# Attention and LayerNorm MLP on one Trainium2 core: the first pair's keys moved to SyncE's queue, the weights g spread in three pieces, and the first attention's list sorted anew

## The chip, the core and the metric

The kernel runs on one core of a Trainium2 chip. A core has five engines, each with its own list of instructions that it works through in order: TensorE (PE in the profile, with its weight loads apart as PEld), VectorE (DVE), ScalarE (ACT), GpSimd (POOL) and SyncE (SP). Engines wait for each other through semaphores. DMA transfers are issued by an engine (SyncE, ScalarE or GpSimd; the profile writes SPq, ACTq, POOLq) into that engine's queue. Operands lie in SBUF, results of matmuls in PSUM.

The metric is the device time of one execution in microseconds (us), as the median over runs of the same kernel.

## The reference

```python
B, H, S, D = 8, 12, 448, 64          # q, k, v: (8, 12, 448, 64) float32; x: (8, 448, 768)
def rmsnorm(x, g):
    return x / sqrt(mean(x * x, -1) + 1e-06) * g
q_n, k_n = rmsnorm(q, g_q), rmsnorm(k, g_k)
attn = softmax(q_n @ k_n.T / sqrt(64))            # per head
x = (attn @ v), heads side by side                # (8, 448, 768)
xn = (x - mean(x)) / sqrt(var(x) + 1e-06) * g_ln
out = x + relu(xn @ w_ch1) @ w_ch2                # w_ch1 768 x 3072, w_ch2 3072 x 768
```

## The kernel before

Heads are worked on in pairs, six pairs to a batch, pairs 0 to 47 in all. Pairs are prepared in units: units 0 to 3 hold pairs 0, 1, 2-3 and 4-5 (batch 0), unit 4 pairs 6-7, and so on; unit 8 holds pairs 14-15. A head's 448 rows are three times 128 "main" rows and 64 "left" rows; the left rows of a pair's two heads share one tile.

**Preparing a pair.** For queries and keys: squares (ScalarE, `square`, L113 and L551), their sums (VectorE, L504), the root (ScalarE, L494/L495), the scaling (VectorE, L515 for keys, L562 for queries). g_q and g_k are only ever used as the product g_q*g_k, `gprod`, which is multiplied onto one side (L555 for the queries of batch 0, the qG steps, and L263 for later keys). Keys are split into a high fp16 half and a low one (steps j and k; L105/L107 and L522), queries are doubled (step m or qm, a copy qn, L568), so that a score is a product of high and low parts at once. Keys and queries are then turned: by TensorE into the PSUM tile `tr` (K steps, L331/L334; Q steps, L348/L351; batch 0's queries into `psQ`, L581), from which a copy brings them to SBUF (C and D steps, QC steps), or by a DMA transpose (steps x and y, L287/L290 for keys and L297/L300 for queries). `tr` exists once: the next K or Q step needs the copy of the one before to be over. Values are cast to fp16 on GpSimd (steps z; L605/L610, later L311/L317).

**Scores, exponentials, values.** S steps are score matmuls, E steps the exponentials on ScalarE (L404, in batch 0 L647), V steps exponentials times values (L441/L443, in batch 0 L668). In batch 0 these go over blocks of query columns, phases 0, 1 and 2 (`S1.3.0` is phase 1, pair 3, half 0; `Q_PARTS` lists which pairs' queries are prepared together); for later pairs `S8.4` is pair 8, seventh part 4. O and T steps scale by the sums and collect the LayerNorm's statistics.

**The MLP.** A and N steps normalise 128 rows, X steps transpose them into `xnT`, U steps are up-projection matmuls of batch 0 (L692, `psU`) and R steps their relu (L700/L702); H steps are the down-projection (L1026, `psC`), J adds x, P stores. For later batches the up-projection is at L992 (`psH`) with its relu at L994. The weights w_ch1 come in three thirds (W0, W1, W2; L899) and w_ch2 in two halves (W3, W4; L904), each issued by GpSimd behind a tiny copy (`poke`, L778) that waits for a load of the inputs. The steps named Y belong to the LayerNorm of batch 1 (Y.X: its DMA transposes, L974).

**What sets the order.** For batch 0's attention and MLP and for batch 1's attention (pairs 6 to 11), with the preparation that lies among them, the order on every engine is the hand-written list `ORDER`: `first_attention` walks it and issues each step to its engine. The table `ENGINE` says which engine does a step that several could do (A ScalarE, V VectorE, P GpSimd; anything not named has a default: VectorE for copies out of PSUM by `moved`, GpSimd for the products qG). `F22` is 22 filler matmuls (L818, `psW`), which multiply the identity with itself and whose result nobody reads. From there on `run_rest` interleaves the MLP of batch b with the attention of batch b + 1 by a planner.

**The loads at the start** are issued ahead of the list, in `load_first`. `key(eng, p)` issues pair p's main key rows on engine `eng`'s queue, `load_left` the left rows (two DMAs, one for each head), `main` queries or values on SyncE's. Before, ScalarE issues pair 0's main keys, pair 0's left rows and pair 1's main keys; SyncE pair 0-1's queries, g_q and g_k (into `gg`), and then the rest; GpSimd the left rows of pairs 1 to 5, after it has built the identity matrix (`make_identity`) for the transposes. `spread_g` multiplies g_q and g_k in one partition (L737), spreads the product over 128 partitions by a matmul with ones (L739, `psG`) and copies it back (L740); it is the first step of `ORDER`.

Of the kernel before, what the change touches and what calls it, by code (L numbers as in the profile page):

```python
# [21 lines left out]
NPAIR = H // 2  # L22
# [5 lines left out]
ENGINE = dict(x.split(":") for x in """ j1:P C1:A QC0.0:A qG0.2:V QC0.2:A QC1.3:A qG2.0:V  # L28
qG2.4:V qm2.4:P QC2.4:A R0.3:V R0.4:V R0.5:V R1.4:V R1.5:V XC2:A R2.0:V R2.2:V R2.4:V c4:P j4:P
m4:P i5:V m5:P j6:P a7:P i7:V j7:P m7:P c8:V j8:P m8:P""".split())  # L30
# [3 lines left out]
spread a0 d0 qa0.0 h0 qt0.0 a1 qG0.0 n0 j0 qg0.0 d1 k0 ql0.0 G L4k qm0.0 h1 F22 K0 n1 a2 C0  # L34
Q0.0 j1 qa1.0 k1 d2 qa0.2 QC0.0 qt0.2 F12 K1 L4q F12 S0.0.0 h2 qt1.0 n2 E0.0.0 a3 C1 L4v qg0.2
j2 S0.0.1 qG0.2 d3 ql0.2 E0.0.1 F30 S0.1.0 h3 qg1.0 qG1.0 qm0.2 F20 Q0.2 E0.1.0 k2 n3 F6 K2
QC0.2 S0.1.1 C2 E0.1.1 ql1.0 j3 F13 S0.2.0 qm1.0 K3 k3 E0.2.0 C3 qa2.0 qt2.0 F7 Q1.3 S0.2.1
Q1.0 E0.2.1 F8 K4 S0.3.0 z0 S0.3.1 W0 V0.0 qa2.4 QC1.3 C4 E0.3.1 F4 K5 qt2.4 qg2.0 QC1.0 E0.3.0
S0.4.0 C5 qG2.0 V0.1 z3 E0.4.0 S0.4.1 qg2.4 E0.4.1 z2 ql2.0 qm2.0 F4 S0.5.0 L5k V0.2 E0.5.0 L5q
F5 S0.5.1 qG2.4 E0.5.1 ql2.4 V0.3 S1.0.0 V0.4 S1.0.1 E1.0.0 V0.5 S1.1.0 Q2.2 E1.0.1 E1.1.0  # L40
S1.1.1 O0.0 T0.0 L6k S1.2.0 W1 O0.1 Q2.0 E1.1.1 E1.2.0 S1.2.1 S1.3.0 V1.0 E1.2.1 S1.3.1 E1.3.0
E1.3.1 V1.1 S1.4.0 S1.4.1 V1.2 E1.4.0 E1.4.1 QC2.0 S1.5.0 V1.3 E1.5.0 T0.1 G2 S1.5.1 V1.4 A0
S2.0.0 E1.5.1 E2.0.0 N0 X0 QC2.2 L5v b4 a4 XC0 S2.0.1 L6v V1.5 qm2.4 O1.0 S2.0.2 O1.1 c4 T1.0
E2.0.2 U0.0 S2.1.0 d4 e4 E2.0.1 V2.0 Q2.4 R0.0 E2.1.0 S2.1.1 S2.1.2 T1.1 QC2.4 E2.1.2 E2.1.1
U0.1 S2.2.0 S2.2.1 g4 A1 V2.1 E2.2.0 S2.2.2 E2.2.1 N1 X1 E2.2.2 l4 S2.3.0 E2.3.0 V2.2 XC1 i4
# [21 lines left out]
BEHIND = {0: (4, 1), 2: (5, 2), 3: (6, 2), 4: (7, 2)}  # L67
PE_SET = (DMA_UNIT + 1) % 2
EARLY = {9: (89, 97)}
PIECES = {x + str(u) for x in "bacdegijklmzxy" for u in range(4, 9)}  # L70
LN_EXP_SET = 6
TWO_LEFT = 5
REC_LO, REC_HI = 1.0 / 3.0e7, 0.5
# [1231 lines left out]
```

## Time and profile before

| | |
|---|---|
| time, median of 3 runs | 598.51 us (597.85 to 599.85) |
| the profiled execution | 599.46 us, of it 597.9 us from the first to the last instruction (span) |
| TensorE busy | 582.4 us, 97% |
| VectorE, ScalarE, GpSimd busy | 296.7, 351.1, 186.2 us |
| granted TensorE clock, mean | 0.999 |

A profile row of the timeline reads: start in us, length in us, engine, line of the kernel, operation, output<-input by the program's names, shapes and types, how many instructions are put together (x3), and in brackets how long the engine had idled before it and whose work ended that. A group's row reads: busy us and mean ns of one, then the idle time before. A matmul's own length includes its way through the array, so that a row's length is more than its distance to the next. Line numbers of the kernel after the change lie a few lines further down (L171 becomes L172, L728 becomes L731).

### The profile page before, as it was taken

To read this page: it belongs to the slowest core of one execution; us is meant where nothing else is said; L and a number is where in the kernel's file an instruction comes from. 1 tells how busy PE (TensorE), PEld (TensorE's weight loads), DVE (VectorE), ACT (ScalarE), POOL (GpSimd) and SP (SyncE) were. 2 spreads that over 40 slices of the span, in tenths; PEclk is the share of its full clock that TensorE was granted. 3 is DMA by queue.
4 is the path that set the end of the run, shared out by engine and by line. 5 is a ranking of instruction groups with operands and counts; after the bars stand their busy time and mean duration, and the time that the engine had idled before them with its cause. 6 is when DMAs were issued, how large, how long until landed. Compare 5 with 4: busy or idle time off the path is not lost.

```text
span 597.9 us, 12462 instructions
## 1 busy us (share of the span) xinstructions
PE 582.4 (97%) x4999; PEld 362.9 (61%) x4999; DVE 296.7 (50%) x645; ACT 351.1 (59%) x668; POOL 186.2 (31%) x250
## 2 busy tenths in 40 slices
PE   5899999999999999999999999999999999999997
PEld 4789886545565666654566656654566666654565
DVE  6999997344455355724256255733356322450011
ACT  5899772188852797358843598538765387114300
POOL 3737251025650555232642345414412000000000
PEclk9999999999999999999999999999999999999999
DMA  8999999727996666946956496749623320040011
GB/s 268 220 243 206 221 230 175 197 51 132 123 178 142 135 96 153 173 128 82 152 130 134 85 125 144 189 105 142 120 63 90 93 63 1 27 107 0 1 53 56
DMA packets 130225, 75.25 MB, mean 126 GB/s; under 512 B 96468, under 2 KB 120356, under 8 KB 130164
## 3 DMA queue, kind: packets, MB, share of 16 engines
q1 hardware_dynamic: 113092, 44.53, 37.5%
q0 software_dynamic: 16128, 29.27, 23.6%
q8 instruction: 40, 0.66, 0.5%
q10 hardware_dynamic: 944, 0.62, 0.4%
q14 instruction: 21, 0.17, 0.1%
HBM read 52.30 MB, written 11.01 MB: 106 GB/s over the span
## 4 chain that ended last, share of the span: by engine, by line
PE 89%; DVE 4%; SPq 2%; ACT 2%; DMA 2%; issue 1%; POOL 0%; POOLq 0%; DVEq 0%
PE psC L1026 36%; PE psH L992 30%; PE psS L383 8%; PE oA L441 5%; PE psU L692 3%; PE oB L443 2%; PE psS L389 1%; SPq L297 1%; PE psS L636 1%; DMA qU<-qn 1%; DMA w<-in_g_k_dram 1%; PE oA L668 1%; PE tr L334 1%; DVE khl L522 0%; ACT E L404 0%
## 5 line engine op out<-in xcount | busy, mean ns | idle before, releaser
L1026 PE MATMUL psC<-w,hT 128*128 128x384 f16 (+1 forms) x1368 | 234.9, 323 | 0.0
L992 PE MATMUL psH<-xnT,w 128*128 128x512 f16 (+1 forms) x1008 | 218.1, 356 | 0.0
L404 ACT ACTIVATE E<-psS,rr_all 128x448 f16<-128x448 f32 x273 | 170.9, 637 | 51.9 <-PE psS L383 50.1
L1026 PEld LDWEIGHTS <-hT 128*128 128x128 f16 x1368 | 127.2, 98 | 78.9 <-issue 4.3
L994 ACT ACTIVATE hT<-psH 128x512 f16<-128x512 f32 (+1 forms) x168 | 93.8, 559 | 129.5 <-PE psH L992 127.8
L992 PEld LDWEIGHTS <-w 128*128 128x128 f16 x1008 | 91.1, 98 | 76.9 <-issue 2.3
L383 PE MATMUL psS<-qU,kU 128*128 128x448 f16 x252 | 86.5, 352 | 1.1 <-DMA qU<-qn 0.5
L441 PEld LDWEIGHTS <-E 128*128 128x128 f16 x819 | 56.3, 98 | 36.1 <-issue 1.6
L1033 DVE SCALAR_TENSOR_TENSOR x<-psC,rs_all,x 128x384 f32<-128x384 f32 x48 | 29.2, 615 | 76.4 <-PE psC L1026 75.9
L263 POOL TENSOR_TENSOR qkv<-qkv,gprod 128x896 f32<-128x896 f32 x18 | 37.7, 2095 | 85.4 <-ACT khl L113 70.0
L441 PE MATMUL oA<-v,E 128*128 128x65 f16 x756 | 58.1, 193 | 0.1
L454 DVE RECIPROCAL rec_all<-oA 128x6 f32<-128x6 f32 x42 | 8.2, 195 | 86.0 <-PE oA L441 85.5
L163 POOL DMA_DIRECT2D qkv<-in_k_dram x14 | 11.2, 797 | 123.6 <-ACT E L404 73.4
L443 PE MATMUL oB<-v,E 128*128 128x65 f16 x252 | 45.3, 193 | 0.1
L255 DVE TENSOR_REDUCE ssq<-khl 128x14 f32<-128x896 f32 x21 | 22.7, 1082 | 44.4 <-ACT khl L113 44.4
L383 PEld LDWEIGHTS <-kU 128*128 128x128 f16 x252 | 24.3, 98 | 17.5 <-issue 1.2
L88 DVE SCALAR_TENSOR_TENSOR qn<-qkv,rr_all 128x256 f16<-128x256 f32 (+2 forms) x71 | 25.2, 415 | 16.9 <-ACT rr_all L259 16.9
L255 DVE TENSOR_REDUCE ssq<-qn 128x14 f32<-128x896 f32 x21 | 22.8, 1084 | 21.3 <-ACT qn L113 21.3
L692 PE MATMUL psU<-xnT,w 128*128 128x128 f16 x432 | 27.1, 219 | 0.0
L443 PEld LDWEIGHTS <-E 128*128 128x128 f16 x273 | 26.3, 96 | 0.4 <-DVE xl L461 0.4
L692 PEld LDWEIGHTS <-w 128*128 128x128 f16 x432 | 25.3, 98 | 1.4 <-issue 0.2
L456 DVE TENSOR_TENSOR x<-oA,rec_all 128x384 f32<-128x384 f32 x42 | 23.4, 558 | 1.3
(160 smaller groups left out, 604.8 us busy)
## 6 DMA issues: line engine op xcount, KB each, us to landing
out_dram<-x SPq DMA_DIRECT2D x20, 384.0 KB, 2.5
qkv<-in_v_dram POOLq DMA_DIRECT2D x15, 384.0 KB, 7.5
qkv<-in_k_dram POOLq DMA_DIRECT2D x14, 384.0 KB, 3.8
qkv<-in_q_dram POOLq DMA_DIRECT2D x14, 384.0 KB, 5.6
w<-in_moe_w_ch_dram POOLq DMA_DIRECT2D x3, 1536.0 KB, 12.5
w<-in_moe_w_ch_dram POOLq DMA_DIRECT2D x2, 2304.0 KB, 25.3
qkv<-in_q_dram SPq DMA_DIRECT2D x7, 384.0 KB, 11.3
qkv<-in_v_dram SPq DMA_DIRECT2D x6, 384.0 KB, 5.8
```

The source lines that it names most:

```text
L88: nc.vector.scalar_tensor_tensor(out=out, in0=x, scalar=8.0, in1=r.unsqueeze(2).broadcast_to([x.shape[0], g, D]), op0=ALU.mult, op1=ALU.mult)
L255: nc.vector.tensor_reduce(out=c["ssq"][:, n], in_=c["sq", n], axis=AX.X, op=ALU.add)
L263: _on(nc, f"i{u}", "P").tensor_tensor(out=self.loads[u][1], in0=self.loads[u][1], in1=sh.gprod.unsqueeze(1).broadcast_to([128, g, D]), op= ...
L383: nc.tensor.matmul(ps[0][:, 0:S], c["main"][:, ts(i, 128)], c["q"][:, ts(h, S)], start=True, stop=True)
L404: self.nc.scalar.activation(out=o, in_=c.pop(("ps", i))[:, 0:S], func=AFT.Exp, scale=self.units[u][3][:, g:g + 1], bias=EXP_BIAS)
L441: nc.tensor.matmul(oA[:, t, cs], E[:, ts(t, 128)], rhs, start=(i == 0 and t == 0), stop=(i == 6 and t == 2))
L443: nc.tensor.matmul(oB[:, cs], E[:, 320:448], rhs, start=(i == 0), stop=(i == 6))
L692: nc.tensor.matmul(ps[:, ts(f, 128)], sh.w1[:, dc, ts(4 * k + f, 128)], self.xnT[:, dc, ts(t, 128)], start=(f == 0 and dc == 0), stop=(f = ...
L992: nc.tensor.matmul(ps[:, 0:N], sh.w1[:, dc, ts(f, 128)], xnT[:, dc, 0:N], start=(dc == 0), stop=(dc == NDC - 1))
L994: nc.scalar.activation(out=hT[:, f, 0:N], in_=ps[:, 0:N], func=AFT.Relu)
L1026: nc.tensor.matmul(self.psC[:, 0:g[1]], self.hT[:, f, ts(t, 128)], sh.w2[:, h, f, c:c + g[1]], start=(f == 0), stop=(f == NFF - 1))
L1033: self.nc.vector.scalar_tensor_tensor(out=x, in0=self.sums.pop((b, t, g[0]))[:, 0:g[1]], scalar=self.rs[:, b, t:t + 1], in1=x, op0=ALU.mul ...
```

## The change

It has four parts.

1. `load_first`: pair 0's and pair 1's main keys are issued on SyncE's queue, pair 0's as the first of all, pair 1's behind the first queries and ahead of g_q and g_k. On ScalarE's queue only pair 0's left rows remain, as the first. `make_identity` stands behind GpSimd's left rows.
2. `spread_g` is cut into three steps of the list: the product (`sp1`, VectorE), the matmul (`spm`, TensorE), the copy (`sp2`, VectorE). They stand behind the first sum of squares (d0), behind h1, and ahead of k0.
3. The cast of values is cut: `z` (in later units `v`) casts the main rows, `za` and `zb` the left rows of the first and the second head.
4. `ORDER` and `ENGINE` are written anew. There are 133 filler matmuls in place of 143. Pair 12's first six scores and exponentials stand in the list. Unit 8's key transposes (x8) stand ahead of its query transposes (y8) and of batch 1's LayerNorm transposes. In `ENGINE`, the copies C2 and C3 go to ScalarE; QC0.2 and QC1.3 from ScalarE to VectorE; the products qG0.2, qG2.0 and qG2.4 and the copies qm0.0 and qm2.0 from VectorE to GpSimd; qG0.0 and qG1.0 from GpSimd to VectorE.

```diff
-ENGINE = dict(x.split(":") for x in """ j1:P C1:A QC0.0:A qG0.2:V QC0.2:A QC1.3:A qG2.0:V
...
+ENGINE = dict(x.split(":") for x in """ j0:P C1:A C2:A C3:A qG0.0:V qm0.0:P QC0.0:A qG1.0:V
...
 ORDER = """
-spread a0 d0 qa0.0 h0 qt0.0 a1 qG0.0 n0 j0 qg0.0 d1 k0 ql0.0 G L4k qm0.0 h1 F22 K0 n1 a2 C0
...
+G L4k a0 qa0.0 d0 sp1 qt0.0 h0 a1 n0 d1 j0 h1 spm sp2 k0 F23 K0 n1 qG0.0 qg0.0 ql0.0 C0 L4q
...
-        key(nc.scalar, 0)
+        key(nc.sync, 0)
         self.load_left(nc.scalar, 1, tk[:, 0:1, 6], 0, 0, 2)
         main(0, tq, 0, 2)
         self.load_left(nc.gpsimd, 1, tk[:, 1:NPAIR, 6], 0, 2, 2 * NPAIR - 2)
-        key(nc.scalar, 1)
+        make_identity(nc, self.sh.id16)
+        key(nc.sync, 1)
         for n in range(2):
             nc.sync.dma_start(self.sh.gg[:, n], self.gs[n].unsqueeze(0))
         key(nc.sync, 2)
...
-                    z=lambda: (vmain(), vleft()))
+                    za=lambda: vleft([0]), zb=lambda: vleft([1]))
...
-    def spread_g(self):
+    def spread_g(self, part):
         nc, sh = self.nc, self.sh
-        nc.vector.tensor_tensor(out=sh.gprod[0:1], in0=sh.gg[:, 0], in1=sh.gg[:, 1], op=ALU.mult)
-        ps = self.ps_m.tile([128, D], FP32, tag="mlp", name="psG")
-        nc.tensor.matmul(ps, sh.row, sh.gprod[0:1], start=True, stop=True)
-        nc.vector.tensor_copy(out=sh.gprod, in_=ps)
+        if part == 0:
+            nc.vector.tensor_tensor(out=sh.gprod[0:1], in0=sh.gg[:, 0], in1=sh.gg[:, 1], op=ALU.mult)
+        elif part == 1:
+            self.psG = self.ps_m.tile([128, D], FP32, tag="mlp", name="psG")
+            nc.tensor.matmul(self.psG, sh.row, sh.gprod[0:1], start=True, stop=True)
+        else:
+            nc.vector.tensor_copy(out=sh.gprod, in_=self.psG)
...
-        for p in range(NPAIR, 2 * NPAIR):
+        for p in range(NPAIR, 2 * NPAIR + 1):
             for i in range(7):
                 ops[f"S{p}.{i}"] = lambda p=p, i=i: self.score(p, i)
...
-        if hp == 0:
+        if b not in self.st:
             st = self.p_m.tile([128, 80], FP32, tag="stat", name="stat", bufs=2)
...
-    make_identity(nc, sh.id16)
```

How instructions stand on the engines shows the moves. First ScalarE from its first DMA to its first squares (hT holds the keys as loaded, qkv the queries; L747 is a warm-up of one column), before:

```order
L163 DMA hT<-in_k_dram 128x2x192
L171 DMA hT<-in_k_dram 64x64 x2
L163 DMA hT<-in_k_dram 128x2x192
L745 ACT_TABLE_LOAD
L747 ACTIVATE warm<-ones 128x1
L113 ACTIVATE khl<-hT 128x448
L551 ACTIVATE qn<-qkv 128x256
```

and after:

```order
L172 DMA hT<-in_k_dram 64x64 x2
L751 ACT_TABLE_LOAD
L753 ACTIVATE warm<-ones 128x1
L114 ACTIVATE khl<-hT 128x448
L553 ACTIVATE qn<-qkv 128x256
```

The left rows lost the key issue in front of them. On SyncE at the same place, before:

```order
L163 DMA qkv<-in_q_dram 128x4x192
L189 DMA w_66<-in_g_q_dram 1x64
L189 DMA w_66<-in_g_k_dram 1x64
L163 DMA hT<-in_k_dram 128x2x192 x2
L163 DMA qkv<-in_q_dram 128x8x192
```

and after:

```order
L164 DMA hT<-in_k_dram 128x2x192
L164 DMA qkv<-in_q_dram 128x4x192
L164 DMA hT<-in_k_dram 128x2x192
L191 DMA w_62<-in_g_q_dram 1x64
L191 DMA w_62<-in_g_k_dram 1x64
L164 DMA hT<-in_k_dram 128x2x192 x2
```

The queries are second and the g's fourth and fifth. VectorE from the product of the g's to the low half of pair 1's keys (hT_124 or hT_120 are the keys, khl their halves, tr the turned keys in PSUM), before:

```order
L737 TENSOR_TENSOR gprod_68<-w2_66 1x64
L740 COPY gprod_68<-psG_159 128x64
L504 TENSOR_REDUCE ssq_162<-khl_165 128x7
L504 TENSOR_REDUCE ssq_168<-qn_171 128x4
L515 TENSOR_TENSOR hT_124<-hT_124,rr_all_164 128x448
L504 TENSOR_REDUCE ssq_176<-khl_179 128x7
L522 TENSOR_TENSOR khl_165<-hT_124,khl_165 128x7x64
L562 TENSOR_TENSOR qn_171<-qkv_128,rr_all_170 128x4x64
L568 COPY qn_171<-qn_171 128x4x64
L515 TENSOR_TENSOR hT_124<-hT_124,rr_all_178 128x448
L728 COPY kT_151<-tr_125 128x960
L522 TENSOR_TENSOR khl_179<-hT_124,khl_179 128x7x64
```

and after:

```order
L506 TENSOR_REDUCE ssq_162<-khl_165 128x7
L741 TENSOR_TENSOR gprod_64<-w2_62 1x64
L506 TENSOR_REDUCE ssq_167<-qn_170 128x4
L517 TENSOR_TENSOR hT_120<-hT_120,rr_all_164 128x448
L506 TENSOR_REDUCE ssq_177<-khl_180 128x7
L746 COPY gprod_64<-psG_187 128x64
L524 TENSOR_TENSOR khl_165<-hT_120,khl_165 128x7x64
L517 TENSOR_TENSOR hT_120<-hT_120,rr_all_179 128x448
L557 TENSOR_TENSOR qkv_124<-qkv_124,gprod_64 128x4x64
L564 TENSOR_TENSOR qn_170<-qkv_124,rr_all_169 128x4x64
L731 COPY kT_151<-tr_121 128x960
L524 TENSOR_TENSOR khl_180<-hT_120,khl_180 128x7x64
```

The product and the copy of psG now stand between the sums and the scalings; the doubling copy is gone and the product qG0.0 (L557) has come. TensorE at K13 (keys of pair 13 turned into tr), before:

```order
L334 MATMUL tr<-id_58,khl 128x128
L334 LDWEIGHTS khl
L334 MATMUL tr<-id_58,khl 128x128
L992 LDWEIGHTS w_72
L992 MATMUL psH<-xnT,w_72 128x512
```

and after:

```order
L336 MATMUL tr<-id_58,khl 128x128
L336 LDWEIGHTS khl
L336 MATMUL tr<-id_58,khl 128x128
L350 LDWEIGHTS qn
L350 MATMUL tr<-id_58,qn 128x2x64
L353 LDWEIGHTS qn
L353 MATMUL tr<-id_58,qn 128x128
```

Pair 13's queries (Q13) are turned into the same tile directly behind its keys. GpSimd from the issue of W2 (the last third of w_ch1) to that of W3 (the first half of w_ch2), before:

```order
L778 COPY poke<-qkv 128x2
L899 DMA w_72<-in_moe_w_ch_dram 128x6x1024
L778 COPY poke<-qkv 128x2
L904 DMA w_66<-in_moe_w_ch_dram 128x24x384
L311 CAST v_112<-qkv 128x12x64
```

and after:

```order
L905 DMA w_68<-in_moe_w_ch_dram 128x6x1024
L310 COPY qn<-qn 128x14x64
L313 CAST v_108<-w_62 128x12x64
L265 TENSOR_TENSOR qkv<-qkv,gprod 128x896
L319 CAST vl<-w_62 64x2x64
L313 CAST v_108<-qkv 128x12x64
L319 CAST vl<-w_62 64x2x64
L108 CAST khl<-qkv 128x14x64
L319 CAST vl<-qkv 64x2x64
L313 CAST v_108<-qkv 128x12x64
L319 CAST vl<-qkv 64x2x64 x2
L784 COPY poke<-qkv 128x2
```

Ten instructions of the preparation now stand between the two issues, and W3's (L910) comes behind the last row. On SyncE around batch 1's LayerNorm transposes (L974, after L980), before:

```order
L297 DMA_TRANSPOSE qU_110<-qn 128x4x128 x3
L300 DMA_TRANSPOSE qU_110<-qn 128x2x64 x2
L171 DMA qkv<-in_v_dram 64x2x64 x2
L974 DMA_TRANSPOSE xnT<-xn 128x6x128 x4
L163 DMA qkv<-in_v_dram 128x4x192
```

and after:

```order
L289 DMA_TRANSPOSE kU_104<-khl 128x12x128
L292 DMA_TRANSPOSE kU_104<-khl 128x2x64 x2
L1048 DMA out_dram<-x 128x384
L172 DMA qkv<-in_v_dram 64x2x64 x2
L980 DMA_TRANSPOSE xnT<-xn 128x6x128 x4
```

Ahead of them stood unit 8's query transposes; now its key transposes do, which before came behind all of batch 0's stores.

More of the change, by code (lines that the diff above doesn't have):

```diff
@@ L40 @@
[L40 to L45, printed above, removed]
@@ new lines @@
+qm0.0 j1 k1 a2 qa0.2 F6 Q0.0 QC0.0 qa1.0 d2 K1 h2 C1 qG0.2 qt0.2 S0.0.0 S0.0.1 z0 qt1.0 za0 z2
+qg0.2 a3 n2 ql0.2 d3 za2 qm0.2 E0.0.1 j2 F42 S0.1.0 zb0 F24 Q0.2 E0.1.0 S0.1.1 k2 qg1.0 K2 h3
+qa2.0 W0 C2 qG1.0 QC0.2 E0.0.0 F16 K3 S0.2.0 n3 E0.1.1 S0.2.1 ql1.0 j3 V0.0 qm1.0 V0.1 k3
+E0.2.1 F10 Q1.0 C3 W1 qt2.0 G2 F8 S0.3.0 L4v E0.2.0 K4 zb2 E0.3.0 S0.3.1 qg2.0 Q1.3 C4 F4
+S0.4.0 K5 z3 QC1.3 E0.3.1 V0.2 S0.4.1 E0.4.0 za3 zb3 qa2.4 C5 QC1.0 qG2.0 V0.3 E0.4.1 S0.5.0
+E0.5.0 O0.0 S0.5.1 S1.0.0 V0.4 E0.5.1 E1.0.0 ql2.0 S1.0.1 S1.1.0 E1.0.1 V0.5 qt2.4 E1.1.0 V1.0
@@ L69 @@
 EARLY = {9: (89, 97)}
-PIECES = {x + str(u) for x in "bacdegijklmzxy" for u in range(4, 9)}
+PIECES = {x + str(u): x for x in (*"bacdegijklmvxy", "za", "zb") for u in range(4, 9)}
 LN_EXP_SET = 6
@@ L864, in attention @@
                     self.prep_ops(u)[y] for y in names
-                    if not {y + str(u), f"z{u}" if y in "vw" else ""} & done)
+                    if not {y + str(u), f"za{u}" if y == "w" else ""} & done)
         steps, mark = [], [0]
```

78 lines of the change are left out of this document (40 added, 38 removed).

## Prediction

> **What bounds the kernel now.** I read the page's head and its chain first, then the span cut into stages, then the fillers and TensorE's waits.
>
> ```profile
> span 597.9 us, 12462 instructions
> PE 582.4 (97%) x4999; PEld 362.9 (61%) x4999; DVE 296.7 (50%) x645; ACT 351.1 (59%) x668; POOL 186.2 (31%) x250
> PE 89%; DVE 4%; SPq 2%; ACT 2%; DMA 2%; issue 1%; POOL 0%; POOLq 0%; DVEq 0%
> ```
>
> ```profile
> 0.00:10.30 10.30, 3.14 (x25) 2.76 (x25) 4.87 (x18) 4.43 (x12) 2.90 (x9) 1.00 0.78 234
> 10.30:20.00 9.70, 8.41 (x118) 7.98 (x118) 9.54 (x14) 8.06 (x19) 4.87 (x5) 1.00 1.12 332
> 20.00:30.00 10.00, 8.89 (x158) 8.02 (x156) 9.96 (x16) 8.57 (x20) 8.69 (x10) 1.00 0.91 170
> 30.00:37.65 7.65, 7.32 (x131) 6.46 (x128) 6.90 (x19) 7.14 (x15) 2.19 (x2) 1.00 1.12 223
> 37.65:50.00 12.35, 12.35 (x225) 11.85 (x223) 12.10 (x20) 11.88 (x25) 7.00 (x10) 1.00 0.93 236
> 50.00:113.77 63.77, 63.66 (x819) 49.36 (x815) 52.46 (x103) 35.52 (x69) 22.05 (x25) 1.00 1.06 198
> 113.77:150.00 36.23, 35.29 (x235) 17.39 (x234) 15.02 (x32) 29.30 (x54) 12.81 (x17) 1.00 0.57 123
> 150.00:597.90 447.90, 443.32 (x3312) 259.04 (x3310) 185.84 (x430) 246.24 (x459) 125.69 (x173) 1.00 0.52 103
> ```
>
> ```profile
> L818 PE MATMUL psW<-id 128*128 128x128 f16 x143 | 11.7, 241 | 0.0
> ```
>
> The columns of the second fence after the stretch and its length are busy us with instruction counts of PE, PEld, DVE, ACT and POOL, then the granted clock and the DMA's share. TensorE is busy 97% of the span and carries 89% of the chain, so time can go only where it idles or where it works on nothing. Up to 37.65 us, where the first big up-projection has just begun, it idles 7.16 + 1.29 + 1.11 + 0.33 = 9.9 us, and the 143 fillers, which compute nothing, take another 11.7. That is the pot, 21.6 us. From 37.65 to 113.77 it idles 0.1 us, from there to 150 us 0.94. After 150 us the order of instructions on TensorE, VectorE and ScalarE is the same in both kernels, so the 4.6 us there stay. The granted clock is 1.00 in each row; I give fewer fillers no price through it.
>
> In the pot it is not TensorE that works. VectorE is busy 9.54 of 9.70 and 9.96 of 10.00 us from 10.3 to 30, ScalarE 8.06, 8.57 and then 7.14 of 7.65. Before 10.3 us everybody waits for the first data. So a shorter start has to come from earlier data, from less VectorE work, or from less ScalarE work.
>
> **The start: the first keys.**
>
> ```profile
> 1.06 0.49 ACTq L163 DMA_DIRECT2D hT<-in_k_dram  x1
> 1.58 1.23 ACTq L171 DMA_DIRECT2D hT<-in_k_dram  x2
> 2.04 0.22 SPq L189 DMA_DIRECT2D w<-in_g_k_dram  x1
> 5.58 0.21 DVE L737 TENSOR_TENSOR gprod<-w 1x64 f32<-1x64 f32 x1 [2.37 <-DMA w<-in_g_k_dram]
> 6.61 0.58 ACT L113 ACTIVATE khl<-hT 128x448 f32<-128x448 f32 x1 [1.63 <-DMA hT<-in_k_dram]
> 7.21 0.62 DVE L504 TENSOR_REDUCE ssq<-khl 128x7 f32<-128x448 f32 x1 [0.42 <-ACT khl L113]
> 10.30 0.29 PE L331 MATMUL tr<-id,khl 128*128 128x128 f16 x1 [1.31 <-DVE khl L522]
> ```
>
> ```profile
> DMA to landing us min/median/max: 4.0/4.1/4.3
> ```
>
> The first square (6.61) waits for pair 0's left rows, two DMAs on ScalarE's queue behind the keys' issue of 0.49 us. Two issues take 1.23 us, so the second starts at 1.58 + 0.61 = 2.2 us; the last line is the landing time of these two, and 2.2 + 4.3 is the 6.5 at which the square could start. With the keys on SyncE's queue the left rows are issued 0.5 us earlier, at 1.06 and 1.67, and land at 5.7 to 6.0. The square starts 0.5 to 0.9 us earlier; I take 0.7. The price on SyncE's queue: the key issue goes ahead of the queries, and another ahead of g, so queries and g leave by one and two issues of about 0.5 us later. The queries then land near 5.8, g near 5.58 + 1.0 = 6.6. Queries are squared after the keys' square (over at about 6.5), and the product of the g's stands now behind the first sum (over at about 7.1), so both lie in cover. If g were later than 7.1, VectorE would stand in front of its own product with K0's scaling behind it, and the gain would be lost microsecond by microsecond.
>
> Fillers ahead of K0 (22 before, 23 after) and the spread of g as matmul and copy now lie later, between h1 and k0. The copy of 64 columns stands on VectorE in front of k0. I bound this by nothing and by the 0.21 us of the product at 5.58, twice, since it is two small instructions that were in idle time and now are not: 0 to +0.4. K0 itself thus hardly moves (10.30 - 0.7 + 0.4), what follows moves by 0.5 to 0.7.
>
> **The start: what changes its engine.** First the rows of VectorE that leave it, and of the others those that price the exchange.
>
> ```profile
> L728 DVE COPY kT<-tr 128x960 f16<-128x960 f16 x3 | 1.9, 648 | 0.0
> L728 DVE COPY qU<-psQ 128x768 f16<-128x768 f16 x3 | 1.6, 545 | 0.0
> L555 DVE TENSOR_TENSOR qkv<-qkv,gprod 128x512 f32<-128x512 f32 x2 | 1.4, 724 | 0.0
> L555 DVE TENSOR_TENSOR qkv<-qkv,gprod 128x256 f32<-128x256 f32 x2 | 0.8, 414 | 0.0
> L555 DVE TENSOR_TENSOR qkv<-qkv,gprod 128x128 f32<-128x128 f32 x1 | 0.3, 285 | 0.0
> L568 DVE COPY qn<-qn 128x256 f16<-128x256 f16 x1 | 0.2, 226 | 0.0
> ```
>
> ```profile
> 22.92 0.86 DVE L568 COPY qn<-qn 128x768 f16<-128x768 f16 x1
> 30.26 0.36 DVE L568 COPY qn<-qn 128x768 f16<-128x768 f16 x1
> ```
>
> ```profile
> 13.03 1.81 POOL L555 TENSOR_TENSOR qkv<-qkv,gprod 128x768 f32<-128x768 f32 x1 [0.99 <-ACT qn L551]
> ```
>
> ```profile
> 15.89 0.95 ACT L726 COPY kT<-tr 128x960 f16<-128x960 f16 x1
> 19.88 1.01 ACT L726 COPY qU<-psQ 128x1024 f16<-128x1024 f16 x1 [0.29 <-PE psQ L581]
> 25.50 0.79 ACT L726 COPY qU<-psQ 128x768 f16<-128x768 f16 x1
> ```
>
> Off VectorE go C2 and C3 (2 x 0.65), all five weight products of the third to sixth rows (1.4 + 0.8 + 0.3) and two copies qn (0.23 and 0.36): 4.4 us. Onto it come QC1.3 (0.55), QC0.2 (1024 columns, 0.73 by the 768 row's rate), qG0.0 (0.41) and qG1.0 (768 columns, 0.724 x 1.5 = 1.09): 2.8 us. Net -1.6 us. ScalarE takes two copies of 0.95 and gives 1.01 and 0.79: +0.1. GpSimd's products grow by 1664 - 1024 = 640 columns, 1.5 us at the rate of 1.81 for 768.
>
> Does VectorE's -1.6 arrive at the first up-projection? Ahead of it stand the exponentials of phases 0 and 1 on ScalarE, which has only 1.64 + 1.43 + 0.51 = 3.6 us of idle time from 10.3 to 37.65, and QC2.4 (0.79) now in front of phase 2's first exponential. A walk through the new list, step by step with these durations, puts the last phase-1 exponential 0.4 us and the first up-projection 0 to 0.7 us earlier (an estimate). Bounds for the whole start: -2.3 us if VectorE's relief and the earlier data both count in full (-1.6 - 0.7), +0.4 if they do nothing and the spread of g is paid. I take the earlier data alone, **-0.7**, since ScalarE's rows are as full as VectorE's from 30 us on, and its sum grows.
>
> The two 768-wide qn copies above are the same instruction at 0.86 and 0.36 us; GpSimd works through the window of the first (its busy share from 20 to 30 us is 87%) and far less in that of the second (2.19 of 7.65 us). The Trainium skill, page "SBUF — State Buffer", section "Who interferes with whom", says that VectorE and GpSimd share one pair of ports under an exclusive lock, and that a VectorE operation with two inputs in SBUF blocks against a GpSimd operation that reads SBUF. This trace agrees in direction with the two copies, 0.86 against 0.36; how much of each of GpSimd's new 1.5 us falls on VectorE no row shows. By the rule in full the relief would be 1.6 - 1.5 = 0.1 us.
>
> Ten fillers fewer at 11.7 / 143 = 0.08 us are 0.8 us of TensorE's time, but they stand in waits for other engines: **0** by themselves.
>
> **The middle, 37.65 to 113.77 us.** TensorE's work is the same and it idles 0.1 us. VectorE and ScalarE are full to 50 us (12.10 and 11.88 of 12.35), so a mis-sorted step there costs at once. I take **0**, with 0.8 us either way, the size of one large copy. The one transfer that can strike is the first half of the down-projection's weights (W3).
>
> ```profile
> 49.54 1.43 POOL L904 DMA_DIRECT2D w<-in_moe_w_ch_dram  x1 [0.27 <-issue]
> ```
>
> ```profile
> DMA to landing us min/median/max: 21.2/25.3/29.4
> ```
>
> ```profile
> 85.49 1.14 PE L1026 MATMUL psC<-w,hT 128*128 128x384 f16 x6
> ```
>
> It lands at 49.54 + 29.4 = 78.9 us, 6.6 ahead of its first reader. GpSimd has ten more instructions between W2 and W3 after the change, while W2 stands earlier; I leave W3 where it is.
>
> **The end of the list, 113.77 to 150 us.**
>
> ```profile
> L404 ACT ACTIVATE E<-psS,rr_all 128x448 f16<-128x448 f32 x22 | 13.7, 633 | 0.0
> ```
>
> ```profile
> 120.11 0.66 DVE L341 COPY kU<-tr 128x960 f16<-128x960 f16 x1 [4.68 <-PE tr L334]
> 124.43 0.95 ACT L113 ACTIVATE khl<-qkv 128x896 f32<-128x896 f32 x1 [0.42 <-DMA kU<-khl]
> 125.95 0.38 PE L389 MATMUL psS<-qU,kU 128*64 128x448 f16 x2 [0.73 <-ACT E L404]
> ```
>
> At 124.43 a square on ScalarE waits 0.42 us for unit 8's key transpose, the exponential behind it is late, and TensorE waits 0.73 us at 125.95. The change issues that transpose (x8) ahead of Y.X and y8: -0.7. Against it, K13's transposes are now followed at once by Q13's, in the same PSUM tile, which a copy of 0.66 us must empty in between: +0.7, as TensorE has nothing else ahead of Q13. Then six exponentials of pair 12 (6 x 0.633 = 3.8 us) leave a stretch in which ScalarE is busy 29.30 of 36.23 us, into one with 35.52 of 63.77. TensorE's other idle time in this stretch is 0.94 - 0.73 = 0.2, so I take -0.3. The six scores themselves only change places. Together **-0.3**; bounds -1.0 (no new wait) and +0.5 (the new wait in full, half of the old one kept).
>
> **Sum.** -0.7 + 0 - 0.3 = -1.0 us. The profiled execution took 599.46 us (span 597.9 and 1.56 around it), 0.95 above the median 598.51; it would become 598.5. Against the median: 598.51 - 1.0 = **597.5**, its own range 596.1 to 598.7 (the bounds of the start and the end hardly meet).
>
> **Rivals.**
> *VectorE's relief pays in full.* For it: 9.96 of 10.00 us busy from 20 to 30, and K0's wait of 1.31 us at 10.30, which ends on VectorE's scaling. Against: ScalarE has 3.6 us of idle time in all, and would have to give up nearly half. -1.6 - 0.7 - 0.3 = -2.6: 595.9.
> *Nothing is gained.* The left rows land when the DMA engines allow rather than when they are issued, or GpSimd's 1.5 us block VectorE. For it: the 0.86 us copy. Start 0, end -0.3 or 0: 598.2 to 598.5.
> *The down-projection waits for W3 (slower).* TensorE reads W3 earlier after the change: H0.0.0 stands five scores and five value steps earlier (two scores take 0.38 us at 125.95, so ten steps some 2.0 us), and the start gives 0.7. Needed at 85.49 - 2.7 = 82.8. With a flight of 29.4 us it is late from an issue after 53.4, 3.9 us later than now. Ten GpSimd instructions took 7.00 us in the row from 37.65 to 50: issued at 56.5, landed at 85.9, 3.1 us late: 600.6. Against it: GpSimd idles 5.35 us in that row, and W2 stands earlier.
>
> **How the numbers follow.** About 0.3%, 1.8 us, is what a measurement of this kernel can tell from no change, so faster means under 596.7 and slower over 600.3. My forecast gets 0.44 (0.14 of it under 596.7, as the start's bound reaches -2.3), the relief in full 0.28 (all faster), nothing gained 0.08 (0.06 same, 0.02 slower), W3 late 0.12 (slower), and other new waits in a list of this length, such as the y8 transposes or VectorE's g product, 0.08 (slower). Faster 0.42, same 0.36, slower 0.22. The range goes from 594.6 (relief in full with the middle's -0.8 and half of the end's -1.0) to 601.0 (W3 late and 0.4 more); about 0.05 lies below and 0.1 above.
>
> **What would show it.** Right: the first square at 5.7 to 6.1; the product of the g's right behind the first sum with no wait; K0 between 9.9 and 10.4; the first up-projection between 36.8 and 37.5; no wait for the exponential near 125, and one of about 0.7 at Q13's transposes; W3 issued before 53 us and no DMA wait at the first psC. Wrong: an up-projection before 36 us (then VectorE was the bound), VectorE's 896-wide scalings and copies longer than now (then GpSimd blocks it), TensorE idle for more than a microsecond in the middle, or a DMA ahead of psC.

## The result, and the profile after

The change makes no difference that can be measured.

| | before | after |
|---|---|---|
| median of 20 runs | 599.37 us (597.85 to 603.18) | 599.62 us (597.91 to 602.3) |
| ratio after / before | | 1.000, 95% interval 0.9986 to 1.0013 |
| profiled execution | 599.46 us, span 597.9 | 598.46 us, span 596.8 |

The two profiled executions differ by 1.0 us, just the forecast gain, and the medians don't. So the profile of after shown here is one of its better executions (its 20 runs go from 597.91 to 602.3 us), which the repeated profiles below bear out. Its stages, in the columns of the table by stages before:

```profile
0.00:10.30 10.30, 3.41 (x29) 3.29 (x30) 5.68 (x20) 4.54 (x12) 2.79 (x9) 1.00 0.76 238
10.30:20.00 9.70, 8.98 (x136) 8.57 (x134) 9.31 (x13) 8.66 (x20) 4.98 (x7) 1.00 1.09 309
20.00:30.00 10.00, 8.84 (x153) 7.68 (x151) 8.41 (x13) 9.13 (x20) 8.34 (x10) 1.00 0.87 170
30.00:37.65 7.65, 6.29 (x117) 5.78 (x115) 7.51 (x19) 6.21 (x15) 5.78 (x6) 1.00 1.11 224
37.65:50.00 12.35, 11.87 (x218) 11.58 (x216) 11.24 (x16) 10.39 (x22) 8.36 (x9) 1.00 1.05 248
50.00:113.77 63.77, 63.77 (x817) 49.18 (x814) 50.04 (x102) 41.25 (x79) 21.12 (x26) 1.00 1.02 201
113.77:150.00 36.23, 35.16 (x238) 17.35 (x236) 15.49 (x34) 27.97 (x51) 13.91 (x19) 1.00 0.52 119
```

VectorE is less busy from 20 to 30 us (8.41 against 9.96; 1.10 us of the difference is a wait, shown below), and from 30 to 37.65 us GpSimd has become busy (5.78 against 2.19) while TensorE idles more, 1.36 us against 0.33. The timeline says why; these are rows of the start:

```profile
5.49 0.58 ACT L114 ACTIVATE khl<-hT 128x448 f32<-128x448 f32 x1 [1.69 <-DMA hT<-in_k_dram]
6.63 0.20 DVE L741 TENSOR_TENSOR gprod<-w 1x64 f32<-1x64 f32 x1
6.89 0.69 PE L744 MATMUL psG<-gprod,w 1*128 1x64 f32 x2 [6.89 <-DVE gprod L741]
7.51 2.63 PE L824 MATMUL psW<-id 128*128 128x128 f16 x23
8.51 0.63 DVE L524 TENSOR_TENSOR khl<-hT,khl 128x448 f16<-128x448 f32 x1
9.93 0.31 PE L333 MATMUL tr<-id,khl 128*128 128x128 f16 x1
21.25 0.77 POOL L784 COPY poke<-w 128x2 f32<-128x2 f32 x1 [2.55 <-DMA w<-in_k_dram]
29.24 1.53 DVE L564 TENSOR_TENSOR qn<-qkv,rr_all 128x512 f16<-128x512 f32 x2 [1.10 <-POOL qkv L557]
31.79 0.51 PE L583 MATMUL psQ<-id,qn 128*128 128x128 f16 x6 [1.15 <-POOL qn L570]
36.87 1.50 PE L695 MATMUL psU<-xnT,w 128*128 128x128 f16 x24
```

The first square starts at 5.49 (6.61 before). But K0 stands behind 23 fillers, which start at 7.51 and take 2.63 us, since psG now waits for the product of the g's. K0's keys are ready at 8.51 + 0.63 = 9.1, and it starts at 9.93: its row has no wait in brackets, because TensorE is busy with fillers. At 29.24 VectorE waits 1.10 us for a product that GpSimd now makes, and at 31.79 TensorE waits 1.15 us for a copy on GpSimd. The first up-projection is at 36.87, 0.62 earlier than before. At the end of the list Q13 (the transposes of pair 13's queries) waits for the copy that empties `tr`:

```profile
120.29 0.22 PE L350 MATMUL tr<-id,qn 128*128 128x128 f16 x1 [0.75 <-DVE kU L343]
```

### The profile page after: what moved, and what is told of

Read it like the earlier page. It is cut to its first block, busy times and chain, and to the rows that moved or that the text cites. A ratio compares the mean times of both kernels' runs of the same rounds, so it can differ in the third digit from the quotient of the medians.

```text
span 596.8 us, 12445 instructions
## 1 busy us (share of the span) xinstructions
PE 580.5 (97%) x4989; PEld 361.9 (61%) x4989; DVE 292.7 (49%) x638; ACT 353.0 (59%) x671; POOL 189.9 (32%) x254
## 4 chain that ended last, share of the span: by engine, by line
PE 89%; DMA 4%; SPq 2%; ACT 1%; DVE 1%; POOL 1%; issue 1%; ACTq 0%; POOLq 0%
PE psC L1032 36%; PE psH L998 32%; PE psS L385 8%; PE oA L443 5%; PE psU L695 3%; DMA qkv<-in_v_dram 2%; PE oB L445 2%; PE psS L391 1%; SPq L172 1%; DMA w<-in_k_dram 1%; DMA hT<-in_k_dram 1%; SPq L164 0%; PE tr L353 0%; PE tr L336 0%; POOL gln L832 0%
## 5 line engine op out<-in xcount | busy, mean ns | idle before, releaser
L265 POOL TENSOR_TENSOR qkv<-qkv,gprod 128x896 f32<-128x896 f32 x20 | 41.6, 2081 | 92.4 <-ACT khl L114 71.6
L456 DVE RECIPROCAL rec_all<-oA 128x6 f32<-128x6 f32 x42 | 8.2, 196 | 83.3 <-PE oA L443 82.8
```

The lines of the kernel that those rows point to most:

```text
L265: _on(nc, f"i{u}", "P").tensor_tensor(out=self.loads[u][1], in0=self.loads[u][1], in1=sh.gprod.unsqueeze(1).broadcast_to([128, g, D]), op= ...
```

## The experiments

All were run in sets on one chip each, with the kernel before in each set. Ratios are those to the kernel before, with 95% intervals.

### Both kernels again

No edit. Before:

> The kernel before once more, for a second profile and for what two identical kernels differ by. Theory A (the 1.1 us between the two profiled spans, 597.9 and 596.8, belongs to the change): span 597.5 to 598.3, first up-projection at 37.4 to 37.6, a wait for the exponential near 126 us. Theory B (executions of one kernel differ by a microsecond and the profiled ones were drawn from either side): the span can be anywhere from 596.5 to 599, with the same 37.5 for the first up-projection. Ratio of times to before 1.000 within 0.0015 under both.

Measured: ratio 0.9988 (0.9966 to 1.0009), median 599.75, profiled execution 599.42 us, span 597.8. After:

> The changed kernel once more. Theory A: span 596.5 to 597.2, ratio to before 0.998. Theory B: the span lies over 597.3 and the ratio is 1.000 within 0.001, though the first up-projection stands again at 36.8 to 37.0 (0.6 earlier than before) and Q13's transposes wait 0.7 us again: what was gained at the start is there, and is given back behind 150 us or drowned in the spread of executions.

Measured: 0.9997 (0.9976 to 1.0019), median 600.49, profiled execution 600.11 us, span 598.6. And once more, in another set:

> The changed kernel a third time, as the anchor of this set and for a third profile. Theory W (the last third of w_ch1, W2, now has its first reader at 58.4 to 58.6 us instead of 63.3 and lands between 57.2 and 59.5, so that TensorE waits for it in some executions; that is where the start's gain goes): a wait of psU for the weights of 0 to 1.5 us at 58 to 60 us, the first up-projection at 36.8 to 37.0 all the same, ratio to before 0.999 to 1.001. Rival R (the loss is elsewhere, behind 150 us): no wait for the weights here, and the time no better than before.

Measured: 1.0005 (0.9993 to 1.0018), median 599.73, profiled execution 601.88 us, span 600.3.

The two profiles of before lie 0.04 us apart, the three of the changed kernel 3.4 us. That before's two are so close is luck: its 20 runs go from 597.85 to 603.18 us. Theory A (the 1.1 us between the spans is the change's) has fallen. The waits of TensorE for the weights, first in the second profile of after, then in the third:

```profile
59.56 1.51 PE L695 MATMUL psU<-xnT,w 128*128 128x128 f16 x24 [1.17 <-DMA w<-in_moe_w_ch_dram]
```

```profile
61.03 1.51 PE L695 MATMUL psU<-xnT,w 128*128 128x128 f16 x24 [1.37 <-DMA w<-in_moe_w_ch_dram]
```

That is U1.4, the first reader of W2. The rows from 50 to 70 us, in the order before, after, after again, after a third time:

```profile
50.00:70.00 20.00, 19.98 (x334) 17.76 (x331) 19.14 (x35) 17.14 (x33) 10.41 (x11) 1.00 1.19 216
```

```profile
50.00:70.00 20.00, 20.00 (x347) 18.33 (x344) 17.55 (x30) 15.32 (x31) 11.88 (x15) 1.00 1.16 210
```

```profile
50.00:70.00 20.00, 18.64 (x307) 16.59 (x305) 15.72 (x29) 13.47 (x27) 11.50 (x14) 1.00 1.19 215
```

```profile
50.00:70.00 20.00, 17.95 (x302) 16.16 (x299) 16.58 (x31) 13.33 (x27) 12.73 (x16) 1.00 1.17 213
```

TensorE idles 0.0, 1.4 and 2.0 us there in the three profiles of after. What moves from one to the next, in us:

| execution | first square | K0 | first up-projection | W2 lands | its first reader | batch 1's first psC | from there to the end of the span |
|---|---|---|---|---|---|---|---|
| before | 6.61 | 10.30 | 37.49 | 59.17 | 63.28 | 156.49 | 441.4 |
| before again | 6.54 | 10.24 | 37.50 | 61.65 | 63.82 | 156.49 | 441.3 |
| after | 5.49 | 9.93 | 36.87 | 57.24 | 58.62 | 155.49 | 441.3 |
| after again | 5.84 | 10.29 | 36.86 | 59.52 | 59.56 | 157.09 | 441.5 |
| after, third | 6.22 | 10.67 | 37.66 | 60.98 | 61.03 | 159.07 | 441.2 |

Before, W2 lands 2.2 to 4.1 us ahead of its first reader; in the new list the first reader stands about 5 us earlier, and W2's landing sets it in two of three executions. The start varies too. From the first square to K0 it is 3.7 us before and 4.4 to 4.5 us after, in each execution. Over all ten profiled executions below and above whose key issues stand on SyncE's queue the first square lies between 5.49 and 6.64 us, over the four on ScalarE's between 6.54 and 6.61.

The landmark in the last two columns is the first down-projection matmul of batch 1 (psC), in the first profiles of before and of after:

```profile
156.49 1.14 PE L1026 MATMUL psC<-w,hT 128*128 128x384 f16 x6
```

```profile
155.49 1.14 PE L1032 MATMUL psC<-w,hT 128*128 128x384 f16 x6
```

Behind it all five executions take 441.2 to 441.5 us. So what the executions gain (1.0 us) or lose (0.6 and 2.6) lies ahead of it, and rival R, a loss behind 150 us, has fallen for these profiles.

### The queue change alone

```diff
-        key(nc.scalar, 0)
+        key(nc.sync, 0)
...
-        key(nc.scalar, 1)
+        key(nc.sync, 1)
```

on the kernel before:

> The kernel before with the first part of the change alone: both keys' issues on SyncE's queue; the product of the g's still stands ahead of the first sum. Mine: the first square at 5.5 (6.61 before), but g is issued 1.0 us later, so VectorE waits for it until 6.6, the copy of psG is over near 7.6, the first sum follows at 7.6 (7.21), K0 at 10.7 (10.30), first up-projection 37.5 to 38.0, time +0.0 to +0.5 us. Rival: earlier keys pay by themselves: K0 at 9.2 to 9.6, first up-projection below 37.0, time -0.7 us.

Measured: 1.0030 (1.0003 to 1.0057), median 602.01 (600.90 to 604.87); the profiled execution, near the top of these, 604.13 us, span 602.6. The first square is at 5.58 as expected, K0 at 10.49, the first up-projection at 37.13: 1.0 us at the square became a loss of 0.2 at K0. The time then missed my expectation by far, and for a reason that I hadn't in it. These are the square on ScalarE that waits for unit 8's key transposes, the scores behind it, and the stretch they open (columns as above):

```profile
126.13 0.95 ACT L113 ACTIVATE khl<-qkv 128x896 f32<-128x896 f32 x1 [1.75 <-DMA kU<-khl]
127.66 0.38 PE L389 MATMUL psS<-qU,kU 128*64 128x448 f16 x2 [2.06 <-ACT E L404]
```

```profile
126.00:134.00 8.00, 6.34 (x33) 2.77 (x33) 2.17 (x2) 6.32 (x11) 3.37 (x4) 0.79 0.00 0
```

The same stretch of the kernel before again:

```profile
126.00:134.00 8.00, 7.93 (x54) 3.80 (x54) 4.32 (x9) 7.77 (x16) 2.92 (x5) 1.00 0.10 23
```

TensorE waits 2.06 us (0.73 and 0.20 in the two profiles of before), and in the 8 us its granted clock is 0.79 on average, which costs some 1.3 us (an estimate, 0.21 of the 6.34 us busy). Why the transposes came 1 to 1.5 us later on SyncE than in before's two profiles is open. So is another 1.6 us: from batch 1's first psC to the end this execution takes 443.0 us, where the five above take 441.2 to 441.5. How much of this holds for the median, 2.1 us below the profiled execution, the one trace can't tell.

### The queue change undone

```diff
-        key(nc.sync, 0)
+        key(nc.scalar, 0)
...
-        key(nc.sync, 1)
+        key(nc.scalar, 1)
```

on the changed kernel:

> The changed kernel with the two key issues back on ScalarE's queue (the first part of the change undone; g is then issued 1.0 us earlier too). By my prediction: the first square at 6.5 instead of 5.5, K0 at 10.5 to 10.9 instead of 10.0, the first up-projection 0.4 to 0.7 later (37.3 to 37.6). Under theory W this costs little or nothing in time (W2 lands when it lands): 0 to +0.4 us against the changed kernel. Without theory W it costs +0.5 to +1.0.

Measured: 1.0013 (0.9998 to 1.0028), median 599.91 (599.73 for the changed kernel in this set). First square 6.60, K0 11.05, first up-projection 37.88, W2 waited for by 0.53 us. Of the 0.4 us by which the square is later than in this set's profile of the changed kernel, the up-projection shows 0.2 and the median 0.2, within the spread: inside the new list no worth of the queue change is measured, and in the old one it gained nothing at K0.

### W2 issued earlier

```diff
-BEHIND = {0: (4, 1), 2: (5, 2), 3: (6, 2), 4: (7, 2)}
+BEHIND = {0: (4, 1), 2: (5, 1), 3: (6, 2), 4: (7, 2)}
```

> The changed kernel with one entry of a table changed: the tiny copy in front of W2's issue waits for unit 5's keys in place of its values, so that W2 can be issued as soon as GpSimd is free, near 41.4 instead of 44.5 us. Theory W: W2 lands at 55 to 57.5, no wait for the weights at its first reader, 0.7 to 1.2 us less than the changed kernel in the medians and less than before by 0.5 to 1.0 us. Rival R: no wait there in either kernel, times equal within 0.4 us. A third way: unit 5's values or unit 6's loads are delayed by the earlier weights and a wait for them between 45 and 56 us takes the gain.

Measured: 1.0063 (1.0051 to 1.0075), median 603.13. The third way happened. W2 was issued at 44.33 (46.07 in this set's profile of the changed kernel), landed at 57.21, and U1.4 did not wait. But unit 6's values came later, and with them what GpSimd does behind them:

```profile
57.54 0.83 POOL L313 CAST v<-qkv 128x768 f16<-128x768 f32 x1 [4.40 <-DMA qkv<-in_v_dram]
68.55 0.22 PE L350 MATMUL tr<-id,qn 128*128 128x128 f16 x1 [2.80 <-DVE kU L343]
```

W3 was issued at 59.87 instead of 55.73. The load of those values (384 KB) was issued at 45.55 us, 1.2 behind W2, and landed after 11.9 us; in this set's profile of the changed kernel it was issued at 45.26, 0.8 ahead of W2, and landed after 4.0 us. In the rows by stage the DMA's share is 0.87 to 1.19 from 10.3 to 113.77 us in both kernels, so the transfers of this stage share what the DMA engines carry: here a weight that comes earlier makes a load come later. The size of the loss, 3.3 us against before, is that of the medians; the traces show only its places, since the profiled execution of W2 early lies near the low end of its runs (602.09 us) and that of the changed kernel in this set near the top of its own (601.88).

### W2, and W1, in halves

```diff
+            if c in (2,):
+                self.load_w1(1024 * c, 1024 * c + 512)
+                self.load_w1(1024 * c + 512, 1024 * c + 1024)
-            if c < 3:
+            elif c < 3:
                 self.load_w1(1024 * c, 1024 * c + 1024)
```

and the same with (1, 2):

> The changed kernel with W2 as two DMAs of 512 columns each, one behind the other: the same bytes, but the first reader (U1.4) needs only the first half. Theory W: the first half lands at 51 to 55 us, no wait for the weights near 60 us in the profile, 0.5 to 1.3 us less than the changed kernel (599.6 to 600.5 in three sets), so a ratio to before of 0.9975 to 0.9995. Rival R: unchanged, or +0.3 by GpSimd's second issue.

Measured: 0.9995 (0.9987 to 1.0004), median 599.54, profiled execution 599.45 us. The first half landed at 53.92, and U1.4 ran at 59.31 without a wait, with as late a start (first up-projection at 37.45) as before. The stretch is full again:

```profile
50.00:70.00 20.00, 19.86 (x339) 18.11 (x337) 17.30 (x32) 14.63 (x29) 12.70 (x16) 1.00 1.21 208
```

So the cause of the wait is shown: U1.4 waited for the whole of W2, of which it needs the first half. But without the wait nothing is gained on before either: batch 1's first psC is at 156.56 (156.49 before), as the start's gain isn't there in this execution and from the first up-projection to that psC it takes 119.1 us, 119.0 in both profiles of before. The wait's worth in the medians is not separated from zero: the ratio lies at the edge of what theory W expected, and inside the interval of the changed kernel's own.

> As the one before, with W1 in two halves as well; U0.2, the first reader of W1, stands at 42.8 to 44 us and W1 lands between 42.4 and 44.4. Theory W: no wait for weights at either place, another 0 to 0.4 us less. Rival: GpSimd's extra issue (0.9 us) in its busiest stretch delays the cast of values and the products that stand behind it, and the start loses 0.3 to 0.9 us.

Measured: 1.0013 (1.0002 to 1.0024), median 600.19. No wait for weights, but the rival won: the first up-projection is at 37.84, VectorE waits 1.70 us for GpSimd's product at 30.21 (1.09 at 29.82 with W2 alone in halves), TensorE 0.55 us for its cast. One issue more in GpSimd's chain costs what it brings, as far as one trace and two medians 0.65 us apart, with intervals that overlap, can say. The control, the same on the kernel before:

> Control: the kernel before with W1 and W2 in halves. There the first readers stand at 53.2 (W1 landed at 42 to 44) and 63.3 us (W2 landed at 59 to 62). Theory W: nothing to gain, ratio to before 1.000 within 0.001, or up to +0.5 us by the two more issues. Rival (smaller weight transfers help everything, for example the loads beside them): it gains as much as the changed kernel does.

Measured: 1.0009 (0.9986 to 1.0032), as theory W has it: nothing to gain where the readers stand later.

### GpSimd's chain at the start

```diff
-E0.2.1 F10 Q1.0 C3 W1 qt2.0 G2 F8 S0.3.0 L4v E0.2.0 K4 zb2 E0.3.0 S0.3.1 qg2.0 Q1.3 C4 F4
+E0.2.1 F10 Q1.0 C3 W1 qt2.0 qG2.0 F8 S0.3.0 L4v E0.2.0 K4 zb2 E0.3.0 S0.3.1 qg2.0 Q1.3 C4 F4
...
-S0.4.0 K5 z3 QC1.3 E0.3.1 V0.2 S0.4.1 E0.4.0 za3 zb3 qa2.4 C5 QC1.0 qG2.0 V0.3 E0.4.1 S0.5.0
+S0.4.0 K5 z3 QC1.3 E0.3.1 V0.2 S0.4.1 E0.4.0 za3 zb3 qa2.4 C5 QC1.0 G2 V0.3 E0.4.1 S0.5.0
```

and qm2.0 out of the table of engines, so that VectorE does it:

> The changed kernel with the product qG2.0 put on GpSimd ahead of the scaling of g_ln (G2, 2.3 us at 23.71) instead of behind it and the casts, and the copy qm2.0 back on VectorE. Theory G (GpSimd became the link in the chain at the start: VectorE waits 1.10 us for its product at 29.24, TensorE 1.15 us for its copy at 31.79): both waits go, the phase-2 queries turn at about 30.2 instead of 31.79, first up-projection at 35.8 to 36.3 (36.87), time -0.6 to -1.0 us against the changed kernel. Rival S (ScalarE's exponentials set the end of the start): the waits go but the first up-projection stays at 36.7 to 37.0 and the time is unchanged.

Measured: 0.9982 (0.9961 to 1.0003), median 599.20, the lowest of its set. The trace doesn't show the expected gain: VectorE's wait is gone, but the casts of the left values now come behind the product, and the first up-projection is at 37.92:

```profile
27.89 0.22 PE L671 MATMUL oA<-vl,E 128*128 128x130 f16 x1 [1.41 <-POOL vl L612]
32.93 0.51 PE L583 MATMUL psQ<-id,qn 128*128 128x128 f16 x6 [0.92 <-DVE qn L570]
```

Neither theory's times came: the place moved within GpSimd's chain and didn't go. In this execution the copy ahead of W0 also ran at 22.90 (21.25 in the first profile of after) because unit 4's keys landed later, and everything behind it on GpSimd with it. That copy ended at 23.86, and the first up-projection came 14.1 us behind it; in the seven profiles of the changed list with GpSimd's chain as it was it came 14.8 to 15.1 us behind. So the later landing may hide a gain of 0.8 us or so, and theory G is not refuted. U1.4 then found its weights (W2 landed at 59.50, read at 60.47). Whether the low median is real is open; the interval reaches 1.0003.

### Pair 12's scores out of the list

The names S12.0 to S12.5 and E12.0 to E12.5 are taken out of `ORDER`:

> The changed kernel with pair 12's six scores and exponentials taken out of the list again, so that the planner places them as before; K13's and Q13's transposes are then 13 TensorE steps apart. By my prediction's step for the end of the list: Q13's wait of 0.75 us is gone, the exponentials cost 0.3 us again: -0.4 us against the changed kernel. Rival: with the scores back in that stretch ScalarE is late again there, as before the change (a wait for exponentials near 126 us of 0.2 to 0.7), and the sum is 0 to +0.5.

Measured: 1.0005 (0.9996 to 1.0015), median 600.04; the first up-projection at 37.92, and at 61.48 the longest wait for W2, 1.86 us. At the end of the list, the row of this kernel:

```profile
113.77:150.00 36.23, 35.82 (x231) 17.83 (x230) 13.08 (x28) 26.69 (x48) 12.82 (x17) 1.00 0.61 138
```

TensorE idles 0.41 us there, 1.07 in all three profiles of after. Q13's wait is gone, and TensorE waits for ScalarE no more than 0.20 us with the six exponentials back. Together with the halves:

> W1 and W2 in halves, and pair 12's scores out of the list. In the run without halves Q13's wait of 0.75 us went and TensorE lost 0.6 us less between 110 and 150 us. Theory W and the separation of K13 and Q13 together: 0.5 us below the kernel with the halves alone, 1.0 to 2.0 us below before (ratio 0.9965 to 0.9985). Rival: the two don't add, since the transposes for unit 8 come late in their place.

Measured: 0.9993 (0.9985 to 1.0002), median 599.42. It is 0.8 us below the kernel with the halves alone, more than expected, but not the 1.0 us or more below before. The profiled execution, the slowest of its 11, had a bad start: TensorE waited 2.46 us for GpSimd's cast at 28.94, and behind it the granted clock fell:

```profile
29.00:32.00 3.00, 2.70 (x39) 2.46 (x39) 1.01 (x3) 2.22 (x5) 2.85 (x5) 0.80 1.13 214
32.00:35.00 3.00, 2.66 (x38) 2.40 (x36) 2.96 (x7) 2.05 (x6) 1.99 (x4) 0.63 1.13 215
```

None of the versions beats both kernels beyond its interval.

## Why the prediction was right and wrong

The time lies 2.1 us above the forecast 597.5 and inside the range; the size of the gain (-1.0 us, a ratio of 0.9983) lies just outside the measured interval. Of the 2.1 us, 0.9 is the start of the sum: before's median is 599.37 over 20 runs and was 598.51 over three. The rest is the gain that didn't come. That the time lies in the range is owed to the range's width, 594.6 to 601.0, and not to the forecast's mechanism; the outcome is that of the rival *Nothing is gained*, which I had given 0.08. By the steps:

- *The first keys, -0.7 at the square.* Right in sign, with a spread that the one profile of before could not show: the first square came at 5.49, 5.84 and 6.22 in the three profiles of after, 0.3 to 1.1 earlier, and at 6.64, with nothing gained, in the kernel without pair 12's scores, whose loads are issued alike. So far that rival was right that the landing doesn't follow the issue. What spreads the landings is open. The g's were in cover, as worked out: their product ran at 6.63 without a wait.
- *K0 and the fillers.* That the fillers "stand in waits for other engines: **0** by themselves" is a step that failed. It counted the fillers and not where the list puts them. Behind a psG that starts at 6.89 to 7.6, the 23 fillers ended after K0's keys were ready (9.1 against 9.93 in the first profile), and from the square to K0 it took 0.75 us longer in each execution (4.44 against 3.69). The spread's two small instructions on VectorE, priced at 0 to +0.4, cost nothing: the keys were ready 3.65 us behind the square, 3.63 before. (`ENGINE` also moves j0, the high half of pair 0's keys, from ScalarE to GpSimd and j1 the other way, which neither the list of the change nor the prediction names; it was over at 8.48 us, ahead of the low half at 8.51.) Fewer fillers at that place weren't tried.
- *The exchange of engines.* That VectorE's -1.6 us would not arrive was right (the sum holds, though the five products stand in the third to fifth rows and not to the sixth); the cover that I named was not. ScalarE itself waited (1.06 us for VectorE at 31.27 in the first profile). GpSimd, which I had gone past with "+1.5 us of products", stands in the chain in the first and third profiles: VectorE waits 1.10 and 1.57 us for its product, TensorE 1.15 and 1.24 for its copy. There GpSimd stands behind the landing of unit 4's keys: its copy ahead of W0 ends at 22.02 and 22.74, and the first up-projection follows 14.9 us behind both times. In the profiles of before that copy ran at 20.57 and 22.23, and the first up-projection stayed at 37.49 and 37.50. The second profile of after reaches 36.86 another way: VectorE comes to the product without a wait, as its own work ahead of it took longer, the same copy first and second (the low half of keys behind it took 1.73 us both times, 1.08 in the third):

```profile
22.01 0.36 DVE L570 COPY qn<-qn 128x768 f16<-128x768 f16 x1
```

```profile
22.59 1.03 DVE L570 COPY qn<-qn 128x768 f16<-128x768 f16 x1
```

  Two profiles of variants are like the second (the queue change undone and no pair 12: copies of 0.98 and 0.99 us, no wait for the product). From the first square to the first up-projection it is 30.88 and 30.96 us before and 31.38, 31.02 and 31.44 after: the earlier square was the whole gain, and the new engines and the fillers together gave back 0.1 to 0.6 of it. The start's -0.7 was thus -0.6, -0.6 and +0.2.
- *The middle, 0 with W3 as the only transfer that can strike.* This is the step that failed most. W3 did what the step says: issued at 54.84, past the point that I had worked out for the rival, it still landed at 77.42 because its flight was 22.6 us instead of 29.4, and the first psC at 82.72 (82.8 worked out) did not wait. These are W3's issue and the first psC in the profile of after:

```profile
54.84 1.47 POOL L910 DMA_DIRECT2D w<-in_moe_w_ch_dram  x1
```

```profile
82.72 1.14 PE L1032 MATMUL psC<-w,hT 128*128 128x384 f16 x6
```

  But the list had pulled forward the first readers of W1 (53.2 to 42.8 us) and of W2 (63.3 to 58.6), and I checked neither against its landing, though each was in the trace and the rows by stage, which I quoted, show the DMA engines at 0.91 to 1.12 of their time from 10.3 to 113.77 us. W2 costs 0, 1.17 and 1.37 us in the three profiles, W1 0.3 in the third. The rival's mechanism was right, its transfer wrong.
- *The end of the list, -0.3.* Q13's new wait is 0.75 (0.7 forecast) and the wait at 125.95 is gone. But that wait was 0.73 us in one profile of before and 0.20 in the other, and the six exponentials that left the stretch brought nothing (0.41 us idle with them back). TensorE's idle time there went from 0.94 and 0.40 to 1.07: +0.1 to +0.7 instead of -0.3.
- *VectorE blocked by GpSimd*, by the rule of the Trainium skill, page "SBUF — State Buffer", section "Who interferes with whom": the traces show the two ways mixed. The 896-wide scalings and low halves of keys, which have two inputs in SBUF, before and after (mean ns behind the busy us):

```profile
L515 DVE TENSOR_TENSOR hT<-hT,rr_all 128x896 f32<-128x896 f32 x2 | 2.6, 1286 | 0.0
L522 DVE TENSOR_TENSOR khl<-hT,khl 128x896 f16<-128x896 f32 x2 | 2.3, 1126 | 0.0
```

```profile
L524 DVE TENSOR_TENSOR khl<-hT,khl 128x896 f16<-128x896 f32 x2 | 2.8, 1402 | 0.0
L517 DVE TENSOR_TENSOR hT<-hT,rr_all 128x896 f32<-128x896 f32 x2 | 2.3, 1128 | 0.0
```

  The one grew and the other shrank, 0.2 us more in all, so the 1.5 us by the rule in full didn't come in this profile. The copy of 0.36 and 1.03 us above ran while GpSimd issued W0 and W1; in the second profile it ended as GpSimd's scaling of g_ln had begun. Whether GpSimd held it up is not shown, since in the first profile the copy ran beside the issue too.

Sum: -0.6, -0.6 and +0.2 at the start. From the first up-projection to batch 1's first psC it is 119.0 us in both profiles of before and 118.6, 120.2 and 121.4 after: -0.4, +1.2 and +2.4, of which the waits for weights are 0, 1.2 and 1.7. Together -1.0, +0.6 and +2.6 at that psC, and behind it nothing. The medians show no change. That these steps, in these shares, make up the medians is argued from three profiles and not shown by an experiment: the halves took the wait for W2 away, and the medians hardly moved.

## What to carry to other kernels

When an order moves work forward, look up for each transfer when it lands and who reads it first in the new order; where the DMA engines are as full as here, that landing does not come forward with the reader, and asking for it earlier can delay another (W2 early: +3.3 us). One profile shows one execution: a gain of the size of what landings vary by needs a second and a third profile of each kernel, with the times of the same landmarks beside each other. Fillers cost nothing only where the wait they fill is longer than they are.

## What had not been expected

Behind a single wait of some 2 us TensorE's granted clock was down, where the first profiles of before and after have it at 1.00 in every 10 us: 0.79 over the 8 us from 126 us, in which a wait of 2.06 us ended, 0.80 and 0.63 in the two 3 us stretches behind a wait of 2.46 us. Behind waits of 1.17, 1.37 and 1.86 us it was 1.00, and so it was behind one of 2.80 us in the kernel with W2 early, so the length of the wait alone doesn't decide.
